# Another order for the opening of a LayerNorm, 2D-FFT filter and gated MLP kernel, with a later chunk's statistics put ahead of a transform

## The chip, the cores and the metric

The kernel runs on one core of one Trainium2 chip. The metric is device time in microseconds (us), the median over runs of the same program; lower is better. The engines are named as in the profile: PE (TensorE, matrix products), PEld (its weight loads), DVE (VectorE), ACT (ScalarE), POOL (GpSimd) and SP (SyncE, whose queue issues the DMA loads, stores and transposes). Each engine works through its own list in order; a step that needs another engine's result waits for a semaphore, and so does everything listed behind it on that engine.

## The reference

The input x has 2048 rows and 448 columns, the inner width is 1792, and everything is in float32:

```python
xn = (x - mean(x)) / sqrt(var(x) + 1e-5)                 # per row
X = rfft2(xn, axes=(-2, -1)) * (w_r + 1j * w_i)
spectral = irfft2(X, s=(2048, 448), axes=(-2, -1))
gate = xn @ W_gate                                       # 448 x 1792
gate = gate * (gate > 0)
mlp = (gate * (xn @ W_up)) @ W_down                      # 1792 x 448
return x + spectral + mlp
```

## The kernel before

**Precision.** All large products run on PE in float16. Each operand is split into a hi part (rounded to float16) and a lo part (what the rounding left), and a product is three passes, hi·hi, lo·hi and hi·lo, added up in PSUM. So for each operand some engine makes hi, and then DVE makes lo by a subtraction that reads hi.

**Tiling.** The 2048 rows are 16 tiles of 128, numbered 0 to 15. Four tiles with the same remainder modulo 4 make a chunk of 512 rows; the chunks are used in the order 0, 2, 1, 3 (`CHUNKS`), so chunk 1 is the third. T0, T2, T1 and T3 are their normalized and transposed forms, what PE streams in the MLP. The gate and up weights come in 14 slabs of 128 inner columns, each as a gate half (g0) and an up half (g1): W0g0, W0g1, W1g0 and so on.

**Steps for one row tile n.** `lx` loads it (SP, `load_xr`). `st` is `ln_stats`: `bn_stats` and `bn_aggr` on DVE, lines 255 and 258 (the profile calls the tile `y`, or `g` for tile 4, which travels in another buffer). `sq` and `rs` are `ln_sd` (one small operation on ACT, line 266) and `ln_rstd` (a chain of four small ones on DVE, 271 to 275). `xn` normalizes on DVE (297), `ax` does the same on ACT (295). `hi` makes the hi part on ACT from the normalized tile (306), or fused with the normalization (`hx` and `hi` stand for the two forms, 304 and 306; for tiles 0, 4, 8 and 12 `hi` is the fused one). `cp` copies two pieces on POOL (310, 311). `lo` is two subtractions on DVE (321 for 384 columns, 322 for 64). The tile then goes to T in one of two ways. For the first chunk PE transposes it: `tpA` the three hi blocks, `tpB` the five other blocks, lo ones among them, all eight into one PSUM tile, and `vevA`/`vevB` or `aevA`/`aevB` bring three and five blocks to SBUF, by DVE or by ACT (345). For the other chunks a DMA transposes it (`dm`, `ln_dma`, line 330 on SP).

**Steps for one weight half.** `lw` loads the next one (SP, line 231, into one of eight `wst` buffers). `wsq` squares it on ACT and sums along the row (185, output `junk`), `parW` sums over the partitions on POOL (188), `wscW` derives a power-of-two scale (two small DVE operations, 191 and 195), `whi` makes hi on ACT (699), `wlo` makes lo on DVE (703) and lets the `wst` buffer go.

**Products.** PSUM has three pairs of banks for the MLP. The products of slab 0 and slab 1 with T0 are cut into small pieces, since neither T0 nor the weights are complete: `hh`, `lh`, `hl` for slab 0 and `ah`, `bh`, `ch` for slab 1, 256 columns at a time (757, 128x256). `gu2g0`, `gu2g1` and on are whole halves of 512 columns. Slab 2 takes the bank pair of slab 0 again: gate after `re0` (ReLU on ACT, 799) has read it, up after `tm0` (the product with up on DVE, 803). `gh` and `gl` split the result again (807, 811), and line 834 is the product with the down weights. `warm` and `kw` are products of a constant (line 1094) whose result nobody reads.

**What sets the order.** The opening, up to about 40 us, is a string of 238 names, `OPENING`. Its steps are issued word by word in a scope where no scheduler moves them, so the string gives each engine's list. What follows is placed by a planner: MLP units in a fixed order, and between them background steps from a list `bg` that is filled in lines 909 to 960: loads of the third chunk's rows, the forward transform of chunk 0 (`fft_chunk`, `f_dft` and on; on DVE lines 385 to 455), its rows, `ln_chunk(1)` (statistics, reciprocal deviation, normalization, lo and transposes of the third chunk), and so on. Each entry has a DVE cost, and the planner spreads the list over the units by those costs. `t_ninth` and `n0` copy what sticks out of T's blocks into a further tile Tl by four small DMAs (351, 352).

Of the kernel before, what the change touches and what calls it, by code (L numbers as in the profile page):

```python
# [33 lines left out]
tpB12 wsqW3g0 vevB8 wloW1g0 ah10 wsqW3g1 vevB12 ah01 parW2 ah11 lwd2 wloW1g1 wscW2 bh00 hl11 hl01 lx14 whiW2g0
bh01 hp0 ch10 whiW2g1 lw st2 bh11 st6 re0 wloW2g0 bh10 wsqW4g1 ch00 ch11 tm0 gu2g0 parW3 wscW3 st14 wsqW4g0
whiW3g0 wloW2g1 ch01 ly0 parW4 wscW4 whiW3g1 wloW3g1 lw wsqW5g1 lx10 whiW4g0 wloW3g0 gh0 re1 st10 gu2g1 tm1 hp2
sqC rsC wsqW5g0 xn6 gu3g0 re2 parW5 wscW5 whiW5g0 tm2 wloW4g0 xn10 xn14 hx14 lwd4 hx6 lo6 hi10 whiW5g1 lo10
gu4g0 hx2 wloW5g0 whiW4g1 cp14 xn2 wdq0 gl0 cp10 gu3g1 wloW4g1 lo14 lwd3 wdq4 wdq2 cp2 re3 tm3 cp6 wloW5g1 gh1
gu4g1 gh2 wdq3 ly12 lo2 hp4 wdq1 wdp wdsc wdh4 dm10 gl1 re4 ly8 wdh3 gl2 gu5g1 tm4 gh4 dm14 gl4 dm6 gu5g0 dm2
re5 lfd gz0g0 wdl3 gz0g1 tm5 hp6 gh3 gl3 rz0 gh5 wdl4 gl5 wdh1 wdl1 wdh2 wdl2 n0 wdh0 wdl0 gz1g0 tz0 gz1g1 rz1  # L40
hz0 tz1 hz1 lz0 lz1
# [103 lines left out]
def tile_gfnet_reglu(ctx: ExitStack, tc: tile.TileContext, x, xr, xi, wgu, wd, wf, c_fd, c_fm, c_im, c_row, c_id,  # L145
# [106 lines left out]
    def ln_stats(q, j):  # L252
        n2 = q + 4 * j
        st = ft([128, 6], F32, "bst", 2)
        V.bn_stats(st, xr_t[n2])  # L255
# [12 lines left out]
    def ln_rstd(q, js=(0, 1, 2, 3), bias=False):
        w, m = rst[q, js[0]]
        r0, t, r, nm = (w[:, i] for i in range(4))  # L270
        V.scalar_tensor_tensor(t, m[:, :, 1], 1e-5, r0, op0=OP.add, op1=OP.mult)
        V.scalar_tensor_tensor(t, t, -0.5 * 2048, r0, op0=OP.mult, op1=OP.mult)
        V.scalar_tensor_tensor(r, t, 1.5 * 2048, r0, op0=OP.add, op1=OP.mult)
        if bias:
            V.scalar_tensor_tensor(nm, m[:, :, 0], -1.0, r, op0=OP.mult, op1=OP.mult)
# [4 lines left out]
    tts = [ft([128, 8, 128], F16, f"tt{i}") for i in range(4)]  # L280
# [15 lines left out]
        else:  # L296
            V.tensor_scalar(xn[n2], xr_t[n2], mean, r, op0=OP.subtract, op1=OP.mult)

    def ln_hi(n2, fused=False):
        new_tt(n2)  # L300
        o = tt[n2].rearrange("p a b -> p (a b)")[:, 0:D]
        r, nm, _ = rst[n2 % 4, n2 // 4]
        if fused:
            A.activation(o, xr_t[n2], AF.Identity, scale=r, bias=nm)  # L304
        else:
            A.activation(o, xn[n2], AF.Copy)
# [387 lines left out]
        for i, k in enumerate(gs):  # L694
            wsc[f, k] = sc[:, i:i + 1]

    def w_hi(f, g):
# [1 line left out]
        A.activation(w[:, 0:4, :], wst[f, g], AF.Copy, scale=wsc[f, g])  # L699
# [392 lines left out]
    def keep_warm(n):  # L1092
        for _ in range(n):
            P.matmul(wps, warm[:, 0:128], warm, start=True, stop=True)
# [192 lines left out]
```

## Time and profile before

| | us |
|---|---|
| median of 3 runs | 442.78 |
| lowest to highest | 442.63 to 443.31 |
| span of the profiled execution | 440.9 |
| busy in it: PE | 435.7 |
| DVE | 382.3 |
| ACT | 184.5 |
| POOL | 29.4 |

The profile is one execution. Its span, 440.9 us, is counted from its first instruction to its last, and what the device needs around it is not part of it, so it stands 1.9 us under the median. Starts in the rows are us from the span's start; a row gives start, duration, engine, line, operation, output <- input, shape, how many were merged into it, and in brackets how long the engine sat idle and who released it. The duration of one instruction overlaps the next one's start on the same engine, so the distance between starts is the cost when they stand back to back. Semaphore events of the trace give the landing of each piece of a load, which the views print only indirectly.

### The profile page before, as it was taken

The page shows a single profiled execution, that of the slowest core. Times are in us where ns is not written, and L with a number is a line of the kernel's source. Part 1 is how long each engine was busy: PE and PEld are TensorE (multiplying, and loading weights), DVE is VectorE, ACT ScalarE, POOL GpSimd, SP SyncE. Part 2 cuts the span into 40 slices and gives each one's busy share as a digit, 9 for nine tenths or more (in the row PEclk, how much of TensorE's full clock was granted, in tenths as well). Part 3 has the DMA queues.
Part 4 walks back from the last instruction along what each step waited for, and adds up shares of the span by engine and source line. Part 5 has one row for each costly group of instructions (what it writes and reads, how often), then busy time and mean ns, then how long its engine had stood idle before and what let it go on. Part 6 is the DMA issues. An engine that isn't in the chain of part 4 may idle for free.

```text
span 440.9 us, 7429 instructions
## 1 busy us (share of the span) xinstructions
PE 435.7 (99%) x2641; PEld 221.9 (50%) x2641; DVE 382.3 (87%) x957; ACT 184.5 (42%) x396; POOL 29.4 (7%) x75
## 2 busy tenths in 40 slices
PE   8999999999999999999999999999999999999996
PEld 3744464554445545444545444444545555555664
DVE  6998496989887879999999999988997989798644
ACT  6995427392457236144023467233113332243220
POOL 3230002011100040000000020000000000000000
PEclk9999999999999999999999999999999999999999
DMA  7929895304111123332220210001111121210212
GB/s 256 301 91 198 269 364 172 70 2 107 59 49 50 47 76 119 94 118 84 86 84 1 84 43 1 0 1 42 44 43 49 54 91 34 72 55 33 89 51 104
DMA packets 37613, 39.55 MB, mean 90 GB/s; under 512 B 16535, under 2 KB 33353, under 8 KB 37577
## 3 DMA queue, kind: packets, MB, share of 16 engines
q1 hardware_dynamic: 37576, 39.09, 29.1%
q8 instruction: 20, 0.33, 0.3%
q14 instruction: 17, 0.13, 0.1%
HBM read 24.38 MB, written 3.67 MB: 64 GB/s over the span
## 4 chain that ended last, share of the span: by engine, by line
PE 90%; DVE 4%; ACT 3%; DMA 1%; issue 1%; SPq 0%; POOL 0%; ACTq 0%
PE bank L757 49%; PE bank L834 27%; PE bank L764 3%; PE fx L648 2%; PE fx L369 2%; PE fx L667 2%; PE fx L406 2%; PE bank L853 2%; ACT wt L699 1%; DMA T<-tt 1%; ACT junk L185 1%; DVE bst L255 1%; DVE wt L703 1%; DMA y<-in_xr 1%; ACT tt L304 1%
## 5 line engine op out<-in xcount | busy, mean ns | idle before, releaser
L757 PE MATMUL bank<-T,wt 128*128 128x512 f16 (+1 forms) x1160 | 252.7, 372 | 0.6 <-DVE T L345 0.5
L757 PEld LDWEIGHTS <-wt 128*128 128x128 f16 x1160 | 110.9, 98 | 127.6 <-issue 7.2
L834 PE MATMUL bank<-wdt,h 128*128 128x448 f16 x624 | 122.4, 352 | 0.0
L834 PEld LDWEIGHTS <-h 128*128 128x128 f16 x624 | 60.5, 98 | 55.1
L799 ACT ACTIVATE g<-bank 128x512 f32<-128x512 f32 x56 | 33.0, 591 | 80.4 <-PE bank L757 45.2
L807 ACT ACTIVATE h<-g 128x512 f16<-128x512 f32 x56 | 35.0, 627 | 70.1 <-DVE g L803 70.0
L803 DVE SCALAR_TENSOR_TENSOR g<-bank,g 128x512 f32<-128x512 f32 x56 | 38.2, 683 | 11.9 <-PE bank L757 6.8
L811 DVE TENSOR_TENSOR h<-g,h 128x512 f16<-128x512 f32 x56 | 38.1, 684 | 6.7 <-ACT h L807 6.4
L840 DVE SCALAR_TENSOR_TENSOR xy<-bank,dsc,xy 128x448 f32<-128x448 f32 x44 | 29.8, 676 | 5.5 <-PE bank L834 5.2
L632 ACT ACTIVATE vt<-y,fsc 128x456 f16<-128x456 f32 x15 | 10.1, 674 | 34.5 <-issue 14.0
L699 ACT ACTIVATE wt<-wst,wsc 128x512 f16<-128x512 f32 x28 | 19.3, 713 | 11.1 <-DVE wsc L195 10.3
L703 DVE SCALAR_TENSOR_TENSOR wt<-wst,wsc,wt 128x512 f16<-128x512 f32 x28 | 20.4, 742 | 0.5 <-ACT wt L699 0.3
L672 DVE SCALAR_TENSOR_TENSOR xy<-fx,fsc,xy 128x448 f32<-128x448 f32 x16 | 10.8, 680 | 10.9 <-PE fx L667 10.9
L188 POOL PARTITION_ALL_REDUCE wm<-wm x15 | 10.5, 697 | 139.9 <-ACT junk L185 136.4
L185 ACT ACTIVATE junk<-wst 128x512 bf16<-128x512 f32 x28 | 17.2, 616 | 0.0
L397 ACT ACTIVATE Xh<-X 128x456 f16<-128x456 f32 x16 | 9.3, 579 | 16.4 <-DVE X L395 9.3
L764 PE MATMUL bank<-T,wt 64*128 64x512 f16 x112 | 15.6, 380 | 0.0
L400 DVE TENSOR_TENSOR Xh<-X,Xh 128x456 f16<-128x456 f32 x16 | 9.8, 624 | 4.9 <-ACT Xh L397 4.9
L648 PE MATMUL fx<-im,vt 128*128 128x128 f16 x192 | 13.3, 219 | 0.0
L667 PEld LDWEIGHTS <-pgh 114*128 114x128 f16 x192 | 10.9, 98 | 3.8 <-issue 0.8
L648 PEld LDWEIGHTS <-vt 128*128 128x128 f16 x192 | 11.6, 98 | 1.3
L406 PE MATMUL fx<-Xh,fm 128*128 128x456 f16 x48 | 12.2, 356 | 0.0
(168 smaller groups left out, 480.1 us busy)
## 6 DMA issues: line engine op xcount, KB each, us to landing
wst<-in_wgu SPq DMA_DIRECT2D x28, 256.0 KB
sw<-y SPq DMA_DIRECT2D x56, 112.2 KB
wf<-in_wf SPq DMA_DIRECT2D x16, 228.0 KB
xy<-in_x SPq DMA_DIRECT2D x16, 224.0 KB
y<-in_xr SPq DMA_DIRECT2D x15, 224.0 KB
out<-xy SPq DMA_DIRECT2D x15, 224.0 KB
wdst<-in_wd SPq DMA_DIRECT2D x14, 224.0 KB
fm<-in_c_fm SPq DMA_DIRECT2D x4, 256.0 KB
```

What stands on the lines that cost most here:

```text
L185: A.activation(mt([128, 512], BF16, "junk", 2)[:, 0:src.shape[-1]], src, AF.Square, scale=SQ, accum_out=acc)
L648: P.matmul(o, v[:, h, w], m[:, c, :], start=(i == 0), stop=(i == 2), skip_group_check=True)
L699: A.activation(w[:, 0:4, :], wst[f, g], AF.Copy, scale=wsc[f, g])
L703: V.scalar_tensor_tensor(w[:, 4:8, :], st, sc, w[:, 0:4, :], op0=OP.mult, op1=OP.subtract)
L757: last["P"] = P.matmul(hps[f, q][g][:, cs], wt[f, g][:, a, :], Tq[q][:, b, cs], start=(start and i == 0), stop=(stop and i == len(seq) - 1 ...
L764: m = P.matmul(hps[f, q][g][:, 0:512], wt[f, g][rows, 7, :], Tq[q][rows, b, :], start=start, stop=stop).ins
L799: last["A"] = A.activation(g1s[f, q], hps[f, q][0], AF.Relu, scale=2.0 ** -22).ins
L803: last["V"] = V.scalar_tensor_tensor(g1, hps[f, q][1], 2.0 ** -22, g1, op0=OP.mult, op1=OP.mult).ins
L807: A.activation(ht[f, q][:, 0, :], g1s[f, q], AF.Copy)
L811: V.tensor_tensor(h[:, 1, :], g1s.pop((f, q)), h[:, 0, :], op=OP.subtract)
L834: last["P"] = P.matmul(ps[:, 0:D], ht[f, q][:, a, js], wdt[f][:, b, :], start=(i == 0), stop=(i == n - 1)).ins
L840: last["V"] = V.scalar_tensor_tensor(xy[:, n2, :], dps[n2][:, 0:D], dsc[:, g:g + 1], xy[:, n2, :], op0=OP.mult, op1=OP.add).ins
```

## The change

All 238 steps of the opening stay, some in another form, and the loads stay in the order they had on SP up to the last few; the order of the steps on the engines is a new one. The first words, before and after, show the kind of edit:

```diff
-OPENING = """lx0 st0 lx4 st4 sqA rsA ax4 hi0 lx8 st8 lx12 xn0 lw cp0 lw lw lw hx4 warm tpA4 st12 tpA0 lo0 lx6 sqB rsB cp4 lo4
-wsqW0g0 tpB0 kw4 tpB4 wsqW0g1 lx2 hi8 parW0g0 wscW0g0 lwd1 whiW0g0 vevA0 parW0g1 wscW0g1 vevA4 hh00 tpA8 whiW0g1
+OPENING = """lx0 lx4 st0 st4 warm18 lx8 lx12 sqA rsA lw vh4 cp4 lw ax0 wsqW0g0 xn4 st12 tpA4 lo4 hx0 parW0g0 tpA0 lw cp0 tpB4 lo0
+tpB0 lw wscW0g0 lx6 wsqW0g1 vevA0 aevA4 parW0g1 wsqW1g0 warm4 lx2 wsqW1g1 aevB4 vevB0 lwd1 wscW0g1 vwW0g0 whiW0g1
...
-    rst = {}
+    rst, rsb = {}, {}
...
-        w = ft([128, 4, 4], F32, "rs", 3)
+        w = ft([128, 4, 4], F32, "rs", 4)
...
-    def ln_hi(n2, fused=False):
+    def ln_hi(n2, fused=False, eng=None):
...
-        if fused:
+        if eng is not None:
+            eng.tensor_scalar(o, xr_t[n2], mean, r, op0=OP.subtract, op1=OP.mult)
+        elif fused:
...
-    def w_hi(f, g):
+    def w_hi(f, g, eng=None):
...
-        A.activation(w[:, 0:4, :], wst[f, g], AF.Copy, scale=wsc[f, g])
+        if eng is None:
+            A.activation(w[:, 0:4, :], wst[f, g], AF.Copy, scale=wsc[f, g])
+        else:
+            eng.tensor_scalar(w[:, 0:4, :], wst[f, g], wsc[f, g], None, op0=OP.mult)
...
-    def ln_chunk(q):
+    def ln_head(q):
         for j in range(4):
             add(0.73, ln_stats, q, j)
         add(0.0, ln_sd, q)
         add(0.75, ln_rstd, q, (0, 1, 2, 3), True)
+
+    def ln_rows(q):
...
     add(0.0, t_ninth, 2)
+    ln_head(1)
     fft_chunk(0)
     fft_rows(0)
-    ln_chunk(1)
+    ln_rows(1)
...
-    ln_chunk(3)
+    ln_head(3)
+    ln_rows(3)
```

Three kinds of step change engine or form. `vh4`, `vh8` and `vh10` make a row tile's hi part on DVE. `vwW0g0`, `vwW2g1` and `vwW4g0` make a weight half's hi part on DVE. `aevA4`, `aevB4`, `aevA8` and `aevB8` evict transposes on ACT instead of DVE, and several normalizations (`xn`) become ACT's (`ax`), while tile 4's becomes DVE's. The constant products are 18 and 4 where they were 21 and 4. `n0`, the four small DMAs for T0, comes earlier. The rest of the diff gives names to further forms of these steps that the string does not use. Outside the opening, `ln_head(1)`, the third chunk's statistics and reciprocal deviation, is taken out of `ln_chunk(1)` and put ahead of the first transform.

ACT's list from the first normalization on, before (`tt_100` is row tile 0's hi and lo, `tt_101` row tile 4's; `junk,wm<-wst` is the square of a weight half):

```order
L295 ACTIVATE y_67<-g_127,rs 128x448
L304 ACTIVATE tt_100<-y_66,rs 128x448
L306 ACTIVATE tt_101<-y_67 128x448
L266 ACTIVATE rs<-mv,eps 128x2
L185 ACTIVATE junk,wm<-wst 128x512 x2
L304 ACTIVATE tt_102<-y_68,rs 128x448
L699 ACTIVATE wt<-wst,wsc 128x512 x2
```

And now (`tt_101` is row tile 0's here, and the L347 row the eviction of transposes of tile 4):

```order
L297 ACTIVATE y_69<-y_66,rs 128x448
L183 ACTIVATE junk,wm<-wst 128x512
L310 ACTIVATE tt_101<-y_69 128x448
L183 ACTIVATE junk,wm<-wst 128x512
L347 ACTIVATE T_62<-fx 128x3x128
L183 ACTIVATE junk,wm<-wst 128x512 x2
L347 ACTIVATE T_62<-fx 128x5x128
L704 ACTIVATE wt<-wst,wsc 128x512
```

The first square of a weight half now stands ahead of row tile 0's hi part, and row tile 4's hi part has left ACT.

DVE's list up to the operands of the first product, before (from the first lo pair's successor on):

```order
L321 TENSOR_TENSOR tt_101<-y_67,tt_101 128x384
L322 TENSOR_TENSOR tt_101<-y_67,tt_101 128x64
L191 TENSOR_SCALAR eg<-wm 128x1
L195 TENSOR_SCALAR wsc<-eg 128x1
L345 COPY T_62<-fx 128x3x128
```

And now (L706 is `vwW0g0`, the first weight half's hi part):

```order
L325 TENSOR_TENSOR tt_101<-y_69,tt_101 128x384
L326 TENSOR_TENSOR tt_101<-y_69,tt_101 128x64
L189 TENSOR_SCALAR eg<-wm 128x1
L193 TENSOR_SCALAR wsc<-eg 128x1
L349 COPY T_62<-fx 128x3x128
L349 COPY T_62<-fx 128x5x128
L189 TENSOR_SCALAR eg<-wm 128x1
L193 TENSOR_SCALAR wsc<-eg 128x1
L706 TENSOR_SCALAR wt<-wst,wsc 128x512
L253 BN_STATS bst<-y_67 128x6
```

Row tile 0's five-block eviction and the second half's scale now stand ahead of the first weight hi part, which was ACT's.

DVE's list around `tm0` (the row with the bank pair's second bank, `bank_112`), before:

```order
L258 BN_AGGR mv<-bst 128x2
L703 SCALAR_TENSOR_TENSOR wt<-wst,wsc,wt 128x512
L803 SCALAR_TENSOR_TENSOR g_404<-bank_112,g_404 128x512
L191 TENSOR_SCALAR eg<-wm 128x2
L195 TENSOR_SCALAR wsc<-eg 128x2
L255 BN_STATS bst<-y_75 128x6
```

And now (`y_75` is row tile 14 and `y_76` row tile 10, so its row is `st10`):

```order
L710 SCALAR_TENSOR_TENSOR wt<-wst,wsc,wt 128x512
L253 BN_STATS bst<-y_75 128x6
L256 BN_AGGR mv<-bst 128x2
L710 SCALAR_TENSOR_TENSOR wt<-wst,wsc,wt 128x512
L253 BN_STATS bst<-y_76 128x6
L256 BN_AGGR mv<-bst 128x2
L810 SCALAR_TENSOR_TENSOR g_428<-bank_112,g_428 128x512
```

The statistics of row tiles 14 and 10 have moved from behind `tm0` to ahead of it.

More of the change, by code (lines that the diff above doesn't have):

```diff
@@ L34 @@
[L34 to L38, printed above, removed]
@@ L39 @@
[L39 to L41 removed]
+OPENING = """lx0 lx4 st0 st4 warm18 lx8 lx12 sqA rsA lw vh4 cp4 lw ax0 wsqW0g0 xn4 st12 tpA4 lo4 hx0 parW0g0 tpA0 lw cp0 tpB4 lo0
+tpB0 lw wscW0g0 lx6 wsqW0g1 vevA0 aevA4 parW0g1 wsqW1g0 warm4 lx2 wsqW1g1 aevB4 vevB0 lwd1 wscW0g1 vwW0g0 whiW0g1
+parW1 st8 sqB wscW1 hh00 wloW0g0 whiW1g1 hl00 ly4 lw rsB vh8 hh10 hl10 lw whiW1g0 lh00 lw ah10 cp8 ch10 ah00 tpA8 hi12
@@ new lines @@
+wloW1g1 tpA12 wloW0g1 bh10 ax12 ch00 aevA8 lw vevA12 wloW1g0 lw lh10 bh11 lw cp12 hh11 wsqW2g1 lo12 bh00 ax8 wsqW2g0
+lo8 tpB12 lwd0 parW2 wsqW3g1 bh01 lwd2 hh01 lx14 vevB12 tpB8 wsqW3g0 wscW2 st6 ah11 parW3 ah01 st2 aevB8 lw whiW2g0
+vwW2g1 lh11 lh01 wsqW4g1 hl11 wsqW4g0 wscW3 hl01 wloW2g0 st14 ly0 hp0 ch01 lw re0 wloW2g1 parW4 lx10 st10 ch11 wsqW5g0
+lwd4 wdq0 tm0 gu2g0 re1 whiW3g1 sqC tm1 wscW4 whiW3g0 gh0 wloW3g1 wloW3g0 lwd3 gu2g1 gl0 wsqW5g1 parW5 n0 ly12 whiW4g1
+hp2 gh1 rsC vwW4g0 re2 ax6 ax10 gu3g1 tm2 wscW5 gu3g0 hi6 gh2 whiW5g1 wloW4g0 lo6 vh10 wloW4g1 ax2 wloW5g1 cp6 hi2
@@ L42 @@
+whiW5g0 cp2 gu4g0 re3 wdq3 hx14 cp10 lo10 gl1 ly8 ax14 lo2 wloW5g0 dm6 gu4g1 cp14 dm10 tm3 hp4 wdq1 wdq2 gu5g1 lo14
+wdq4 wdp gl2 dm2 re4 gu5g0 tm4 gh4 dm14 gh3 wdsc wdh3 wdh0 gl4 re5 tm5 wdh1 wdh2 gz0g0 gz0g1 wdl1 hp6 wdh4 wdl2 gz1g0
+gl3 wdl4 rz0 gh5 gz1g1 rz1 tz0 gl5 wdl3 wdl0 tz1 lfd hz0 hz1 lz0 lz1
 """
@@ L255, in ln_stats @@
         V.bn_stats(st, xr_t[n2])
-        if j == 0:
+        if q not in mv:
             mv[q] = ft([128, 4, 2], F32, "mv", 2)
         V.bn_aggr(mv[q][:, j, :], st)
-    rst = {}
+    rst, rsb = {}, {}
     def ln_sd(q, js=(0, 1, 2, 3)):
-        w = ft([128, 4, 4], F32, "rs", 3)
+        w = ft([128, 4, 4], F32, "rs", 4)
         n = len(js)
-        rst[q, js[0]] = w[:, :, 0:n], mv[q][:, js[0]:js[-1] + 1, :]
-        A.activation(w[:, 0, 0:n], rst[q, js[0]][1][:, :, 1], AF.Abs_reciprocal_sqrt, bias=eps)
+        rsb[q, js[0]] = w[:, :, 0:n], mv[q][:, js[0]:js[-1] + 1, :]
+        A.activation(w[:, 0, 0:n], rsb[q, js[0]][1][:, :, 1], AF.Abs_reciprocal_sqrt, bias=eps)
     def ln_rstd(q, js=(0, 1, 2, 3), bias=False):
-        w, m = rst[q, js[0]]
+        w, m = rsb[q, js[0]]
         r0, t, r, nm = (w[:, i] for i in range(4))
@@ L274, in ln_rstd, with ln_bias @@
         if bias:
-            V.scalar_tensor_tensor(nm, m[:, :, 0], -1.0, r, op0=OP.mult, op1=OP.mult)
+            ln_bias(q, js)
         for i, j in enumerate(js):
             rst[q, j] = r[:, i:i + 1], nm[:, i:i + 1], m[:, i, 0:1]
+    def ln_bias(q, js):
+        w, m = rsb[q, js[0]]
+        V.scalar_tensor_tensor(w[:, 3], m[:, :, 0], -1.0, w[:, 2], op0=OP.mult, op1=OP.mult)
     xn, tt, xn_b = {}, {}, {}
@@ L1096, in tile_gfnet_reglu @@
     pieces = {"lfd": lambda: nc.sync.dma_start(fd_t, c_fd),
-              "lw": load_wn, "warm": lambda: keep_warm(NWARM),
-              **{f"kw{n}": (lambda n=n: keep_warm(n)) for n in (1, 3, 4)},
+              "lw": load_wn, **{f"warm{n}": (lambda n=n: keep_warm(n)) for n in range(1, 25)},
               "wdp": lambda: wd_sum(len(groups[0])),
@@ L1110, in tile_gfnet_reglu @@
             n2 = q + 4 * j
+            piece(f"sq{n2}", ln_sd, q, (j,))
+            piece(f"rs{n2}", ln_rstd, q, (j,))
+            piece(f"nm{n2}", ln_bias, q, (j,))
             for tag, fn, *a in (("lx", load_xr), ("ly", load_x), ("st", ln_stats, j), ("xn", ln_xn),
-                                ("hi", ln_hi, c == 0), ("hx", ln_hi, c == 1), ("ax", ln_xn, True), ("cp", ln_copy), ("lo", ln_lo), ("dm", ln_dma),
+                                ("hi", ln_hi, c == 0), ("hx", ln_hi, c == 1), ("ax", ln_xn, True), ("cp", ln_copy), ("lo", ln_lo),
+                                ("vh", ln_hi, False, V), ("dm", ln_dma),
                                 ("tpA", ln_tp, (0, 1, 2)), ("tpB", ln_tp, (4, 5, 6, 3, 7))):
@@ L1151, in tile_gfnet_reglu @@
             piece(f"whiW{f}g{g}", w_hi, f, g)
+            piece(f"vwW{f}g{g}", w_hi, f, g, V)
             piece(f"wloW{f}g{g}", w_lo, f, g)
@@ L1154, in tile_gfnet_reglu @@
             if f == 0:
+                for j in range(2):
+                    for tag, sq in (("hq", seq1[0:3]), ("lq", seq1[3:6]), ("kq", seq2)):
+                        piece(f"{tag}{g}{j}", gu_full, f, q, (g,), slice(128 * j, 128 * j + 128), tag == "hq" and j == 0,
+                              False, sq)
                 piece(f"parW{f}g{g}", w_sum, f, (g,))
```

5 lines of the change are left out of this document (1 added, 4 removed).

## The prediction

> **What bounds the kernel now.** I read the page's busy shares and chain first, then the windows, then each engine's timeline over the opening.
>
> ```profile
> PE 435.7 (99%) x2641; PEld 221.9 (50%) x2641; DVE 382.3 (87%) x957; ACT 184.5 (42%) x396; POOL 29.4 (7%) x75
> PE 90%; DVE 4%; ACT 3%; DMA 1%; issue 1%; SPq 0%; POOL 0%; ACTq 0%
> ```
>
> TensorE (PE) is busy 435.7 of 440.9 us. The windows (length, then busy time of PE, PEld, DVE, ACT, POOL) say where the rest lies:
>
> ```profile
> 0.00:10.00 10.00, 8.78 (x37) 3.78 (x38) 6.28 (x25) 5.74 (x12) 3.76 (x17) 1.00 0.77 241
> 10.00:20.00 10.00, 9.51 (x93) 7.55 (x92) 9.44 (x29) 9.22 (x22) 2.50 (x7) 1.00 0.97 330
> 20.00:30.00 10.00, 10.00 (x56) 4.94 (x55) 9.72 (x28) 9.37 (x21) 1.81 (x5) 1.00 0.34 118
> ...
> 40.00:50.00 10.00, 9.89 (x49) 4.16 (x48) 6.51 (x12) 5.29 (x11) 0.00 (x0) 1.00 0.95 305
> ...
> 80.00:90.00 10.00, 10.00 (x81) 5.32 (x79) 10.00 (x34) 4.55 (x11) 0.00 (x0) 1.00 0.09 24
> ```
>
> From 20 us PE is full, so the main phase can give back almost nothing. The start decides; PE's timeline there:
>
> ```profile
> 1.22 7.46 PE L1094 MATMUL bank<-row_t 128*128 128x512 f16 x21 [1.22 <-DVE row_t L1166]
> 8.52 0.78 PE L337 MATMUL fx<-g,tt 128*128 128x128 f16 x11
> 9.13 1.03 PE L1094 MATMUL bank<-row_t 128*128 128x512 f16 x4
> 9.99 0.44 PE L337 MATMUL fx<-g,tt 128*128 128x128 f16 x5
> 10.93 0.49 PE L757 MATMUL bank<-T,wt 128*128 128x256 f16 x3 [0.49 <-DVE T L345]
> ```
>
> L1094 is warming on constants, L337 the first transposes, L757 the first product: useful work starts at 10.93. After it PE runs nearly without a break, so every microsecond by which the first product moves goes straight into the end, unless a later stall swallows it.
>
> **First product: +0.9.** What comes before it on ScalarE (ACT), SyncE's DMA queue and VectorE (DVE):
>
> ```profile
> 6.02 0.76 ACT L295 ACTIVATE y<-g,rs 128x448 f32<-128x448 f32 x1 [0.81 <-DVE rs L275]
> 6.69 0.75 ACT L304 ACTIVATE tt<-y,rs 128x448 f16<-128x448 f32 x1
> 7.34 0.56 ACT L306 ACTIVATE tt<-y 128x448 f16<-128x448 f32 x1
> ...
> 8.13 0.61 ACT L185 ACTIVATE junk<-wst 128x512 bf16<-128x512 f32 x1
> 8.74 0.61 ACT L185 ACTIVATE junk<-wst 128x512 bf16<-128x512 f32 x1
> ...
> 10.13 1.33 ACT L699 ACTIVATE wt<-wst,wsc 128x512 f16<-128x512 f32 x2
> ```
>
> ```profile
> 2.60 1.85 SPq L231 DMA_DIRECT2D wst<-in_wgu  x4
> ...
> 6.29 0.61 SPq L214 DMA_DIRECT2D xy<-in_x  x1
> 8.01 5.33 SPq L231 DMA_DIRECT2D wst<-in_wgu  x6
> ```
>
> ```profile
> 5.90 0.62 DVE L255 BATCH_NORM_STATS2 bst<-y 128x6 f32<-128x448 f32 x1
> ...
> 6.66 0.48 DVE L297 TENSOR_SCALAR y<-y,mv,rs 128x448 f32<-128x448 f32 x1
> ...
> 7.81 0.58 DVE L321 TENSOR_TENSOR tt<-y,tt 128x384 f16<-128x384 f32 x1
> ...
> 8.47 0.19 DVE L271 SCALAR_TENSOR_TENSOR rs<-mv,rs 128x2 f32<-128x2 f32 x1
> ...
> 9.16 0.55 DVE L321 TENSOR_TENSOR tt<-y,tt 128x384 f16<-128x384 f32 x1
> ...
> 9.76 0.15 DVE L191 TENSOR_SCALAR eg<-wm 128x1 uint32<-128x1 uint32 x1
> ...
> 10.01 0.35 DVE L345 COPY T<-fx 128x384 f16<-128x384 f16 x1
> 10.28 0.14 DVE L191 TENSOR_SCALAR eg<-wm 128x1 uint32<-128x1 uint32 x1
> ```
>
> Before, ACT finishes both rows' hi parts (L304, L306) by 7.90 and only then squares the first weight slab (L185 at 8.13). The change puts that square between row 0's normalization and row 0's hi part, on an engine that works in order. So the row waits for the weights. When do they land? SyncE's next weight load, queued behind the last x load (6.90), starts only at 8.01: its queue slot is that of the first slab, whose last piece the trace's semaphore events put at 7.99. The load's place in the queue is unchanged, so I take 8.0 again.
>
> The walk, by start-to-start distances of the same rows: normalization at 6.02 as before; square 8.02; hi 0.61 later (8.74−8.13), 8.63; its end 9.19 (0.56). The lo pair on DVE follows at 9.22; its first part (0.55) releases the first of the five transposes that need lo, near 9.84, and the five take 0.44 (PE's row at 9.99): 10.28. The first eviction of that row, three blocks of hi, shares its PSUM tile with those five, and in the new program it waits for the tile's last transpose: 10.32 (before, a three-block eviction ran at 10.01). Behind it on DVE, in order: the five-block eviction +0.27 (10.28−10.01) at 10.59; that one takes 0.40 to the next start (0.27 for three blocks, and two more of 128 at a column a nanosecond or less, half of it hidden: an estimate), so the second slab's scale stands at 10.99 and, being two small operations of 0.25 together (10.01−9.76), ends the wait at 11.24; then the first slab's hi part, which now is DVE's. That operation is not in the trace; beside the L297 row above stands:
>
> ```profile
> 11.59 1.40 DVE L703 SCALAR_TENSOR_TENSOR wt<-wst,wsc,wt 128x512 f16<-128x512 f32 x2
> ```
>
> L297, the same operation on 448 elements, took 0.48; two-source ones on 512 took 1.40 a pair, some 0.74 each. I take 0.55 (0.48 scaled by 512/448), bounds 0.48 and 0.74. It ends 11.79; semaphore to PE 0.04: **first product 11.83 against 10.93, +0.90** (+0.83 to +1.09 by the bounds). PE waits through this, so the three dropped warm matmuls (0.22 each) gain nothing.
>
> Whether ACT's new evictions of the other row's tiles matter: an ACT read of PSUM of 512 took 0.58 (quoted below), so 384 and 640 lie near 0.49 and 0.70; they end at 10.3 and 12.2, the second within 0.1 of its first reader. Before, PE lost some 0.1 each at 11.36 and 14.77; I count the small stalls 11 to 15 equal. The Trainium skill ("ScalarE: Activation LUTs", on the cost of an ACTIVATE) gives 186 ns and 0.833 ns an element, so 0.51 and 0.72 here; the trace's 0.58 for 512 lies just under its 0.61. By it nothing in the sum moves.
>
> **The first reuse of a bank: +0.4.** PE, then the load that st10 reads, then DVE, then ACT:
>
> ```profile
> 19.04 6.89 PE L757 MATMUL bank<-T,wt 128*128 128x256 f16 x42
> ```
>
> ```profile
> 18.65 0.43 SPq L225 DMA_DIRECT2D y<-in_xr  x1
> ```
>
> ```profile
> 20.52 0.68 DVE L803 SCALAR_TENSOR_TENSOR g<-bank,g 128x512 f32<-128x512 f32 x1
> ...
> 24.39 0.62 DVE L255 BATCH_NORM_STATS2 bst<-y 128x6 f32<-128x448 f32 x1
> ```
>
> ```profile
> 19.76 0.58 ACT L799 ACTIVATE g<-bank 128x512 f32<-128x512 f32 x1
> ```
>
> L803 (tm0) frees the up bank; gu2g1 writes it next. Of the 42 products from 19.04, eighteen of 256 columns (0.110 apart) come before gu2g0 at 21.02. In the new order a further four (ch01) come first, 0.44: 21.46, and 22.36 with the +0.90. gu2g0's ten of 512 columns (0.216) end at 24.52, when gu2g1 wants the bank. DVE reaches tm0 later than before: twenty steps stand between the hi part at 11.24 and tm0. By distances from start to start: five statistics of 0.76 (6.66−5.90) are 3.80, six weight lo parts of 0.66 (1.40−0.74) 3.96, a chain of four small ones 0.69 (9.16−8.47), two hi parts 0.39 (0.48 less the 0.09 by which neighbours overlap) and 0.50, evictions 0.27 and 0.40, two lo pairs 0.66 (8.47−7.81) 1.32, three scale pairs of two slabs some 0.3 each 0.9: 12.2. From 11.74, when the hi part lets the next start, tm0 starts at 23.9 if DVE never waits, ends 24.6, and PE loses 0.1. But st10 now stands ahead of tm0, and it waits for the load at 18.65, which before was read only at 24.39 (semaphore events: landed 23.16). It is issued at about the same time, with other loads shifted some 2 us around it; I put its landing between 22 and 24, thus the loss between 0 and 1.2. I take 0.4.
>
> **T2's and T1's transposes: −0.28 and −0.13.** The chain and PE's weight loads:
>
> ```profile
> 36.42 3.87 DMA T<-tt
> ...
> 40.33 4.49 PE bank L757 x20
> ```
>
> ```profile
> 80.02 0.10 PEld L369 LDWEIGHTS <-Tl 128*128 128x128 f16 x1
> 80.22 0.56 PEld L757 LDWEIGHTS <-wt 128*128 128x128 f16 x4
> ```
>
> PE stood 0.28 (starts 0.49 apart instead of 0.216) for the last transpose of T2, landed 40.29. The new order issues it near 36.5, so it lands at about the same time, but PE comes 1.3 later: gone. At 80 a load follows its forerunner by 0.20 where 0.05 would do; PE's matmul starts 0.13 late, for T1, whose transposes are the last to land ahead of it. With the third chunk's statistics ahead of the transform, and no row DMAs ahead of them on SyncE, they can start some 10 us sooner: gone. What hides the moved statistics (four of 0.76 on DVE and a chain of four small ones): they begin near 40, where DVE is busy 6.5 of 10 (window row) and nothing behind them is due at once. Without that cover each would hold up what frees a bank by its 0.76. From there to the end PE's order is the same, and the tail with it.
>
> Sum: +0.90 +0.4 −0.28 −0.13 = **+0.89**. Span 440.9 → 441.8. The median 442.78 lies 1.88 above the profiled span; the same distance gives **443.7**. A measurement of this kernel can tell about 0.2% (0.9 us) from no change.
>
> **Rivals.**
>
> *A: the weights land earlier.* Only three of the 16 pieces came after 6.81. If all come by 6.78, the square follows the normalization directly, hi ends 7.95, and the lo pair waits for DVE (about 8.2). The same chain then gives a first product at 10.8 (8.2 in place of 9.22 for the pair), 10.4 if the pair needn't wait: −0.5 to −0.1. It decides from a landing at 7.1 down. With both transposes' gain: about −0.6, so 442.2, between −0.9 and 0; not slower. Against it: the queue and what is on it have not changed, and SyncE's stop until 8.01 is in this profile. 25%.
>
> *B: a queue behind a wait.* Both ACT and DVE are over 90% full from 10 to 30 (window rows); st10's load lands late, or another in-order wait is added to it, and gu2g1 and the product after each lose 0.5 to 1. +1.6 to +2.5: 445.0. 16%.
>
> *C: PE slows down.* PE idles 1.2 us before row 0's transposes (7.87+0.17 to 9.24), and once more before the first product. If that drops the clock to the start's pace, the 21 warm matmuls' row prices it: 7.46 us where 21×0.217 is 4.6, so up to 2.9 more. For it: the start. Against it: 0.49 of idle at 10.93 was followed by full pace. +2.9 and the sum: 446. 4%. The Trainium skill ("TensorE: Matmul & The Clock Gate", Part 1: The HAM clock gate) lets the clock fall only after an idle window of some 3.4 us; by it C is out. No run here shows a gap that long, and the slow start here (about 5.5 us) is longer than its one window.
>
> **Numbers.** Forecast 55%: +0.2 to +1.6, half of it over +0.9. Slower by over 0.2%: 0.27+0.16+0.04 = 0.47. Same: 0.28 of the forecast and 0.14 of A: 0.42. Faster: A's far end, 0.11. Range 442.0 to 445.1: it leaves out A's end, B's upper half and C.
>
> **What would show it.** Right: the square (ACT, `junk`) starts near 8.0 with idle time ahead of it, hi after it, the first L757-kind product near 11.8; a PE wait on `g` from DVE near 24.5; no transpose wait at 40 and 80. Wrong: hi done before 8.4, or the first product under 11.2 (A); any later PE stall over 0.5 (B); products 0.22 apart for 256 columns (C).

## The result, and the profile after

The changed kernel takes 449.19 us (448.44 to 451.03, 5 runs) where the kernel before takes 443.31 (442.63 to 443.85, 5 runs, same chip): ratio 1.0139, interval 1.0123 to 1.0154, so 5.9 us slower. The forecast was 443.7 with a range to 445.1. The sign that had the largest chance came out; the size is outside the range.

The profiled execution spans 447.2 us, 6.3 more than before. Busy shares and chain from the page after:

```profile
PE 437.3 (98%) x2638; PEld 222.2 (50%) x2638; DVE 381.0 (85%) x954; ACT 186.1 (42%) x399; POOL 34.9 (8%) x75
PE 81%; DVE 10%; DMA 5%; issue 1%; ACT 1%; SPq 1%; DVEq 0%; ACTq 0%
```

PE's share of the chain fell from 90% to 81%. DVE and DMA now have 10% and 5% of it, so somewhere PE waits for them. POOL is busy 5.5 us longer with the same 75 instructions. PE's waits in sum, with count and longest:

```profile
PE bank L771 <- DVE g L810: 2.5, 2, 2.2
PE fx L341 <- ACT tt L310: 1.3, 1, 1.3
PE bank L764 <- ACT g L806: 0.8, 1, 0.8
PE bank L764 <- DVE wt L706: 0.6, 1, 0.6
PE fx L341 <- POOL tt L315: 0.3, 1, 0.3
```

The largest one is on a line that did not wait at all before (L764 there, L771 here: the products with Tl). Where they lie, in PE's timeline of the opening:

```profile
1.22 6.72 PE L1105 MATMUL bank<-row_t 128*128 128x512 f16 x18 [1.22 <-DVE row_t L1185]
7.79 0.33 PE L341 MATMUL fx<-g,tt 128*128 128x128 f16 x3
9.42 1.08 PE L341 MATMUL fx<-g,tt 128*128 128x128 f16 x13 [1.31 <-ACT tt L310]
10.34 1.03 PE L1105 MATMUL bank<-row_t 128*128 128x512 f16 x4
11.99 1.04 PE L764 MATMUL bank<-T,wt 128*128 128x256 f16 x7 [0.63 <-DVE wt L706]
```

The first product comes at 11.99 (10.93 before). Later in PE's timeline:

```profile
37.69 4.26 PE L764 MATMUL bank<-T,wt 128*128 128x512 f16 x19
42.71 3.61 PE L764 MATMUL bank<-T,wt 128*128 128x512 f16 x16 [0.76 <-ACT g L806]
...
204.00 0.82 PE L771 MATMUL bank<-T,wt 64*128 64x512 f16 x6 [0.35 <-DVE g L810]
...
231.60 1.18 PE L771 MATMUL bank<-T,wt 64*128 64x512 f16 x6 [2.18 <-DVE g L810]
232.72 6.20 PE L764 MATMUL bank<-T,wt 128*128 128x512 f16 x22
```

and the same place before:

```profile
226.71 0.82 PE L764 MATMUL bank<-T,wt 64*128 64x512 f16 x6
227.46 4.92 PE L757 MATMUL bank<-T,wt 128*128 128x512 f16 x22
```

Two things are new there. PE stands 2.18 us. Then the same 28 products take 1.18 + 6.20 where they took 0.82 + 4.92: 1.64 us for a slower pace, start to start up to 427 ns for 512 columns instead of 216. Windows of the changed kernel show the clock that PE was granted (the first number behind the five busy times, as a share of full speed):

```profile
228.53:231.94 3.41, 1.23 (x9) 0.51 (x8) 3.41 (x8) 0.36 (x1) 0.00 (x0) 1.00 0.46 147
231.94:235.35 3.41, 3.41 (x13) 0.97 (x8) 3.41 (x8) 0.87 (x2) 0.00 (x0) 0.50 0.24 77
```

Half the clock was granted for 3.41 us, right behind 3.41 us in which PE was busy for only 1.23.

The difference between the two traces, by distances from start to start on PE:

| place | us |
|---|---|
| first product, 10.93 to 11.99 | +1.06 |
| small stalls at 12 to 13 | +0.06 |
| 17.9: last transpose of the first chunk, waits for POOL's copy | +0.41 |
| 24.9: `gu2g1` behind `tm0` | +0.25 |
| 41.6: 0.92 of standing, 0.28 before | +0.64 |
| 80: T1's transposes | −0.13 |
| 204: waits for L810 | +0.35 |
| 229 to 239: 2.18 idle, 1.64 slow pace | +3.82 |
| rest | −0.2 |
| span | +6.3 |

The opening and T2 cost 2.3; more than half of the loss comes at 200 to 239, far from anything that the new string holds.

### The profile page after: what moved, and what is told of

Read it like the earlier page. It is cut to its first block, busy times and chain, and to the rows that moved or that the text cites. A ratio compares the mean times of both kernels' runs of the same rounds, so it can differ in the third digit from the quotient of the medians.

```text
span 447.2 us, 7419 instructions
## 1 busy us (share of the span) xinstructions
PE 437.3 (98%) x2638; PEld 222.2 (50%) x2638; DVE 381.0 (85%) x954; ACT 186.1 (42%) x399; POOL 34.9 (8%) x75
## 4 chain that ended last, share of the span: by engine, by line
PE 81%; DVE 10%; DMA 5%; issue 1%; ACT 1%; SPq 1%; DVEq 0%; ACTq 0%
PE bank L764 45%; PE bank L841 23%; PE bank L771 3%; PE fx L652 2%; PE fx L373 2%; PE fx L671 2%; PE fx L410 2%; PE bank L860 2%; DMA wf<-in_wf 2%; DMA wst<-in_wgu 1%; DMA y<-in_xr 1%; DVE y L524 1%; DVE g L810 1%; DVE xy L847 1%; DMA sw<-yx 1%
## 5 line engine op out<-in xcount | busy, mean ns | idle before, releaser
L764 PE MATMUL bank<-T,wt 128*128 128x512 f16 (+1 forms) x1160 | 254.0, 373 | 1.5 <-ACT g L806 0.8
L764 PEld LDWEIGHTS <-wt 128*128 128x128 f16 x1160 | 111.5, 98 | 130.3 <-issue 10.0
L814 ACT ACTIVATE h<-g 128x512 f16<-128x512 f32 x56 | 35.0, 626 | 73.1 <-DVE g L810 73.0
L810 DVE SCALAR_TENSOR_TENSOR g<-bank,g 128x512 f32<-128x512 f32 x56 | 38.3, 686 | 17.6 <-ACT g L806 8.9
L818 DVE TENSOR_TENSOR h<-g,h 128x512 f16<-128x512 f32 x56 | 38.4, 686 | 8.3 <-ACT h L814 8.2
L704 ACT ACTIVATE wt<-wst,wsc 128x512 f16<-128x512 f32 x25 | 17.4, 712 | 13.2 <-DVE wsc L193 9.9
L186 POOL PARTITION_ALL_REDUCE wm<-wm x15 | 11.4, 768 | 138.3 <-ACT junk L183 138.3
L676 DVE SCALAR_TENSOR_TENSOR xy<-fx,fsc,xy 128x448 f32<-128x448 f32 x16 | 10.8, 681 | 10.9 <-PE fx L671 10.9
L771 PE MATMUL bank<-T,wt 64*128 64x512 f16 x112 | 15.9, 386 | 2.5 <-DVE g L810 2.5
L297 ACT ACTIVATE y<-y,rs 128x448 f32<-128x448 f32 x15 | 10.7, 752 | 3.4 <-DVE rs L279 2.1
```

The source lines that it names most:

```text
L764: last["P"] = P.matmul(hps[f, q][g][:, cs], wt[f, g][:, a, :], Tq[q][:, b, cs], start=(start and i == 0), stop=(stop and i == len(seq) - 1 ...
L771: m = P.matmul(hps[f, q][g][:, 0:512], wt[f, g][rows, 7, :], Tq[q][rows, b, :], start=start, stop=stop).ins
L810: last["V"] = V.scalar_tensor_tensor(g1, hps[f, q][1], 2.0 ** -22, g1, op0=OP.mult, op1=OP.mult).ins
L814: A.activation(ht[f, q][:, 0, :], g1s[f, q], AF.Copy)
L818: V.tensor_tensor(h[:, 1, :], g1s.pop((f, q)), h[:, 0, :], op=OP.subtract)
```

## The experiments

Three theories had to be told apart. **The opening theory**: the first product's delay is the price, as the forecast had it. **The late theory (L)**: the planner put the spectral work of the main phase in other places, and that loses time at 200 to 239. **The T2 theory (T)**: what ends the opening is T2's last transpose, held up by POOL. The expectations also name further rivals, each explained where it stands. All times are medians; each ratio is against the kernel before on the same chip, and kernels measured on different chips (the last three on another) are compared by these ratios.

### The third chunk's statistics alone

The old opening in the changed kernel (with `warm21` and `warm4` for the old `warm` and `kw4`):

```diff
-OPENING = """lx0 lx4 st0 st4 warm18 lx8 lx12 sqA rsA lw vh4 cp4 lw ax0 wsqW0g0 ...
+OPENING = """lx0 st0 lx4 st4 sqA rsA ax4 hi0 lx8 st8 lx12 xn0 lw cp0 lw lw lw hx4 warm21 tpA4 ...
```

> The opening of before, with the third chunk's statistics ahead of the first transform as after. After's trace loses 2.4 us up to 60 us (first product +1.06, a POOL copy at 18 +0.41, the up bank at 25 +0.25, a gate bank at 42 +0.92, T2's wait gone -0.28) and about 4 us more between 200 and 236 (DVE idle on late loads, the product of the up half waiting for DVE, and eight products at half pace behind it). Theory S: the statistics ahead of the transform push the whole spectral chain back by their 3.7 us of DVE, and that is what comes due at 200 to 236; then this kernel is some 4 us slower than before (447.0 to 447.6), the first product stays at 10.9, and PE waits near 229. Rival O: the late stall is the opening's doing, by what it leaves to the scheduler; then this kernel is within 0.5 us of before (T1's 0.13 gone).

Measured: 442.61 (441.98 to 443.39, 10 runs), ratio 0.9993 (0.998 to 1.0005). Its waits on PE:

```profile
PE bank L765 <- DVE T L350: 0.7, 1, 0.7
PE bank L772 <- DVE g L811: 0.2, 1, 0.2
```

No wait on T2 or T1 and none of 2 us: the statistics ahead of the transform cost nothing by themselves, and with the old opening the main phase is sound. So the new string, or what it does together with the planner, makes the loss.

### The new opening alone

```diff
-    ln_head(1)
     fft_chunk(0)
     fft_rows(0)
+    ln_head(1)
```

> The new opening, with the third chunk's statistics back behind the first transform. Theory S: the 2.4 us up to 60 us stay, the 4 us at 200 to 236 go: 445.5 to 446.0. Rival O: 449, as after. Should the two halves not add up (with the old opening and the statistics ahead), each needs the other.

Measured: 445.26 (444.37 to 446.39, 5 runs), ratio 1.0054 (1.0036 to 1.0073). The late loss is gone. In the profiled execution the first weight half had landed at 6.98, the case of rival A, and the first product came at 10.81, ahead of before's 10.93. Still:

```profile
38.65 2.54 PE L764 MATMUL bank<-T,wt 128*128 128x512 f16 x11
42.56 2.75 PE L764 MATMUL bank<-T,wt 128*128 128x512 f16 x12 [1.37 <-DMA T<-tt]
```

PE gets to T2 early and stands 1.37 for its transposes, which land at 42.42 (semaphore events). An early first product is given back at T2. Since moving the entry in the list also changes the order of the main phase, this run alone doesn't say what removed the late loss.

### The row's hi part ahead of the first square

```diff
-... lw ax0 wsqW0g0 xn4 st12 tpA4 lo4 hx0 parW0g0 ...
+... lw ax0 hx0 wsqW0g0 xn4 st12 tpA4 lo4 parW0g0 ...
```

> After, with row tile 0's hi part on ACT ahead of the first square of a weight half, which waited for its load until 8.15. The step as predicted (a hi part stuck behind a late load): first product from 11.99 to about 10.9, and as PE is full behind it about 1 us less: 448.1 or so. Rival: the chain through the evictions and the second half's scale on DVE is as late by itself, since the second square now comes later: first product stays over 11.6 and the time within 0.4 of after.

Measured: 449.2 (448.82 to 449.3, 4 runs), ratio 1.014 (1.0125 to 1.0155): as the changed kernel, though its first product is 0.89 earlier in the profile. Most of that is the weights, which landed at 7.44 in this execution (8.16 in the changed kernel's). PE:

```profile
11.10 2.16 PE L764 MATMUL bank<-T,wt 128*128 128x256 f16 x17 [0.63 <-ACT T L347]
...
43.04 2.32 PE L764 MATMUL bank<-T,wt 128*128 128x512 f16 x10 [1.21 <-ACT wdt L738]
```

In all seven profiles of the new opening with the hi part behind the square the first product comes 3.83 or 3.84 after the weights have landed, and in the four with the hi part ahead of it (this one and three below) 3.56 to 3.66. So the edit itself is worth some 0.2, and the rival was near the truth: with the weights at 8.16 the first product would, by that, still come at about 11.8. The row keeps waiting for the weights on POOL, where its two copies (8.86 and 9.01 here) stand behind `parW0g0`, which needs the square.

The opening theory fails as the price of the whole: the wait behind `tm0` at 24 grows from 0.25 to 1.02, the one at 41 from 0.92 to 1.38, and together they eat the earlier start, wherever it came from. The late loss stays (2.04 of idle at 229.7, then the slow pace).

### The last ReLU ahead of the down weights

At 41.6 the named releaser is ACT's `re5`, which stands behind two hi parts of the down weights; the first of these waits for DVE's scale.

```diff
-... gh3 wdsc wdh3 wdh0 gl4 re5 tm5 ...
+... gh3 re5 wdsc wdh3 wdh0 gl4 tm5 ...
```

> After, with the ReLU re5 put ahead of the down weights' scale and their first two hi parts on ACT. In after PE stands 0.92 at 42 until re5 has read the bank. If re5 alone holds it, 0.8 to 0.9 go (448.3). But T2's last transpose was issued at 39.8 and its first piece landed at 42.4, so the rival is that T2 takes over: only 0.2 go, and PE then waits for a DMA.

Measured: 445.24 (444.51 to 445.43, 4 runs), ratio 1.0054 (1.0036 to 1.0071), 4 us under the changed kernel where under 1 us was expected. A miss, and its cause is in the written order: this edit too changes the planner's placing of the main phase, and the late loss is gone. At 41 PE now waits 1.34 for T2 itself, landing at 42.19: the ReLU and T2 had ended within 0.02 of each other, and without one the other decides.

### Only the planner's cost

The opening's string stays word for word; one cost of the background list changes, and with it only the order of the main phase.

```diff
-            add(0.73, ln_stats, q, j)
+            add(0.86, ln_stats, q, j)
```

> After with one number of the planner changed: it books a row tile's statistics at 0.86 us instead of 0.73. No instruction and nothing of the opening changes; only the order of the main phase does. In the written DVE order the third chunk's first spectral sum stands behind 19 MLP units instead of after's 20 and the first filter products behind 26 instead of 28, as they do in the kernels that lost nothing late. Theory L (after's late loss lies in this order, not in the opening nor in the statistics as such): no PE wait near 204 and 229, no half pace behind it, some 4 us less: 444.9 to 446. Rival: the late loss comes from how late the opening ends or from the statistics' 3.7 us: 449, as after.

Measured: 445.77 (445.08 to 445.99, 4 runs), ratio 1.0062 (1.0043 to 1.0081). PE where it stood 2.18:

```profile
229.56 0.82 PE L771 MATMUL bank<-T,wt 64*128 64x512 f16 x6
230.31 4.92 PE L764 MATMUL bank<-T,wt 128*128 128x512 f16 x22
```

No wait, full pace, and 3.4 us less than the changed kernel with the same opening and the same instructions: the late loss lies in the order of the main phase, and L is shown. The other direction, 0.60:

> The same number at 0.60. The written order keeps the spectral chain where after has it (20 units, 28). Theory L: the late loss stays, 448.5 to 449.7. Rival (any nudge to the planner frees it): about 445.

Measured: 448.9 (448.65 to 449.1, 4 runs), ratio 1.0134 (1.0119 to 1.0149). L810 is waited for four times, 3.4 us in sum. PE at the same place:

```profile
231.78 0.82 PE L771 MATMUL bank<-T,wt 64*128 64x512 f16 x6 [1.64 <-DVE g L810]
232.53 4.92 PE L764 MATMUL bank<-T,wt 128*128 128x512 f16 x22
```

Here full pace follows after 1.64 of idle.

What the two orders differ in: in DVE's list the third chunk's first sum of the transform (the fifth of eight such sums in all) stands behind 18 products with up (`tm`, L810) in the changed kernel, in the one with the row's hi part first and in the 0.60 one, and behind 17 before and in every other kernel of this case (the expectations count units of the program, 20 and 19). Those three kernels have the late loss, and no other has it. On the chip the sum starts at 137.6 in the changed kernel, 131.9 before, 130.6 in the kernel with the old opening, and 132.9 with cost 0.86. From there the spectral chain runs some 5 to 7 us behind that of the 0.86 kernel. How it reaches PE, back from the stall: DVE, ACT and SP of the changed kernel:

```profile
217.55 0.69 DVE L818 TENSOR_TENSOR h<-g,h 128x512 f16<-128x512 f32 x1 [2.17 <-ACT h L814]
```

```profile
215.81 0.30 ACT L517 ACTIVATE wf<-wf 128x114 f32<-128x114 f32 x1 [4.96 <-DMA wf<-in_wf]
...
216.91 0.61 ACT L814 ACTIVATE h<-g 128x512 f16<-128x512 f32 x1
```

```profile
211.75 0.90 SPq L513 DMA_DIRECT2D wf<-in_wf  x2
```

The filter load `wf` stands on SP behind the spectral rows' transfers, is issued at 211.75 (202.27 with cost 0.86, 201.64 before) and lands at 215.8. ACT works in order: the sign flip L517 waits for it, the gate's hi part L814 stands behind L517, and DVE's L818 behind L814 stands 2.17. DVE then works without a break until L810 at 230.86, which PE has waited for since 229.4: 2.17 lost on DVE, 2.18 on PE. In the other two kernels with this loss the same two waits are 2.03 and 2.04 (row's hi part first) and 1.64 and 1.64 (0.60). This path is read from the traces; no run moved that one load alone. Before, the same flip on ACT waited for nothing:

```profile
207.72 0.47 ACT L513 ACTIVATE wf<-wf 128x114 f32<-128x114 f32 x2
```

### The opening without the late loss

With cost 0.86, the row's hi part first again:

```diff
-            add(0.73, ln_stats, q, j)
+            add(0.86, ln_stats, q, j)
...
-... lw ax0 wsqW0g0 xn4 st12 tpA4 lo4 hx0 parW0g0 ...
+... lw ax0 hx0 wsqW0g0 xn4 st12 tpA4 lo4 parW0g0 ...
```

> The planner's number at 0.86, and row tile 0's hi part ahead of the first weight square on ACT. If the first product is on the path, as the prediction had it, the time falls by what the first product gains against the kernel with the number alone, 0.1 to 1.0 by when the weights land. Theory T: T2's transposes and the ReLU re5 hold PE at 41 to 42.5 whatever comes before, since other engines set their time, so the first product is worth nothing: within 0.3 of the kernel with the number alone, and the PE wait near 41 longer by what the start gained.

Measured: 445.13 (444.9 to 446.62, 4 runs), ratio 1.0057 (1.0035 to 1.0078). Inconclusive: 0.6 under the kernel with 0.86 alone, and the intervals overlap. Its profile is of the slowest of the runs, with the weights at 8.03 and the first product at 11.68 (7.90 and 11.73 with 0.86 alone), and PE waits 1.3 behind `tm0` and 0.8 for T2.

### T2 and POOL

Why is T2 late? POOL's copies in the changed kernel, each of 48 or 64 columns:

```profile
16.04 0.22 POOL L314 COPY tt<-tt 128x48 f16<-128x48 f16 x1
16.20 2.03 POOL L315 COPY tt<-tt 128x64 f16<-128x64 f16 x1
...
33.25 1.88 POOL L314 COPY tt<-tt 128x48 f16<-128x48 f16 x1 [1.67 <-ACT tt L310]
35.07 0.73 POOL L315 COPY tt<-tt 128x64 f16<-128x64 f16 x1
...
35.91 0.23 POOL L315 COPY tt<-tt 128x64 f16<-128x64 f16 x1
36.09 0.22 POOL L314 COPY tt<-tt 128x48 f16<-128x48 f16 x1
36.25 1.35 POOL L315 COPY tt<-tt 128x64 f16<-128x64 f16 x1
```

and DVE beside the last three:

```profile
35.63 0.68 DVE L810 SCALAR_TENSOR_TENSOR g<-bank,g 128x512 f32<-128x512 f32 x1
36.23 0.54 DVE L325 TENSOR_TENSOR tt<-y,tt 128x384 f16<-128x384 f32 x1
36.69 0.22 DVE L326 TENSOR_TENSOR tt<-y,tt 128x64 f16<-128x64 f32 x1
36.83 0.68 DVE L818 TENSOR_TENSOR h<-g,h 128x512 f16<-128x512 f32 x1
```

A copy takes 0.22 or 0.23 beside L810, whose one source is a PSUM bank, and 1.35 beside L325, L326 and L818, whose two sources are both in SBUF and which follow one another without a gap. In the two traces every copy that took over 0.4 ran beside such an operation. The Trainium skill ("SBUF — State Buffer", SBUF: two separate sides) says that VectorE and GpSimd share a pair of ports under an exclusive lock, which the operation that starts first holds to its end, a VectorE one with two SBUF inputs among them. The trace agrees, and adds that POOL didn't get in between operations that stood back to back: the copy at 16.20 outlasted five of them. The copies at 33.25 and 35.07 are row tile 2's; row tile 10's stand behind them, and SP, whose next transpose is row tile 10's, waits for those:

```profile
SPq L334 <- POOL tt L314: 2.4, 1, 2.4
```

The SP queue is in order, so the four transposes of T2 are issued at 31.64, 36.17, 37.51 and 39.76 (30.80, 33.71, 35.06 and 36.42 before), and the last lands at 42.57 (40.29). Of the 3.3 us by which the last is issued later, 2.5 were there at the second; the rest is the issue of the third, which took 2.09 (1.25 before). Experiment: row tile 10's copies ahead of tile 2's, out of the longest runs of such operations; `re5` early as well; cost 0.86.

```diff
-... wloW5g1 cp6 hi2 whiW5g0 cp2 gu4g0 re3 wdq3 hx14 cp10 lo10 ...
+... wloW5g1 cp6 cp10 hi2 whiW5g0 cp2 gu4g0 re3 wdq3 hx14 lo10 ...
...
-... gh3 wdsc wdh3 wdh0 gl4 re5 tm5 ...
+... gh3 re5 wdsc wdh3 wdh0 gl4 tm5 ...
```

> The planner's number at 0.86, re5 ahead of the down weights' hi parts, and on POOL tile 10's copies ahead of tile 2's, which in after took 1.9 and 0.7 instead of 0.2 each and held tile 10's transpose. Theory T: T2's transposes are issued in a queue that waits for POOL, so their last landing comes 1 to 2 us sooner than 42.4, PE's wait near 41 shrinks from 1.5 to about 0.3, and the time is 443.9 to 444.8. Rival: POOL's copies are held up by DVE wherever they stand; nothing gained, 445.2 to 445.9.

Measured: 444.29 (443.1 to 445.35, 5 runs), ratio 1.0032 (1.0012 to 1.0052). T2's last transpose is issued at 37.19 and lands at 41.10; PE doesn't wait for it. The swap of the copies without the ReLU's:

> The kernel of e5 (planner cost 0.86, 445.77) with row tile 10's two POOL copies ahead of tile 2's, and re5 left behind the down weights. If the POOL copies alone hold T2's last transpose: it is issued near 37 to 38 and lands by 41.5, PE waits near 41 for the ReLU re5 on ACT instead, 0.3 to 0.9, and the time is 445.0, between e5 and e8 (444.3). If the ReLU's place is what e8 gained by: as e5, 445.8.

Measured: 443.98 (443.57 to 445.51, 12 runs), ratio 1.0027 (1.0016 to 1.0038). POOL in this kernel:

```profile
32.95 0.55 POOL L314 COPY tt<-tt 128x48 f16<-128x48 f16 x1
33.45 0.23 POOL L315 COPY tt<-tt 128x64 f16<-128x64 f16 x1
35.23 0.34 POOL L314 COPY tt<-tt 128x48 f16<-128x48 f16 x1 [1.55 <-ACT tt L308]
35.52 0.23 POOL L315 COPY tt<-tt 128x64 f16<-128x64 f16 x1
```

By the ratios the swap alone brings some 1.5 us against the kernel with 0.86 alone (1.0062), give or take 1.0, and no less than the two edits together. That the copies held T2 back is shown: PE doesn't stand at 41 at all. How much it is worth is not shown so finely. The two profiles are 1.8 apart (spans 443.7 and 441.9); 0.8 of that is the wait for T2, and 1.0 is a shorter wait behind `tm0` near 25, ahead of anything that the swap touches. The expected wait for the ReLU did not come. All four kernels with 0.86 and the swap have the same order in the main phase as the one with 0.86 alone.

### What is left in the opening

The kernel with both edits, and the row's hi part first; then also `st10` back behind `tm0` and `tm1`:

```diff
-... ax0 wsqW0g0 xn4 st12 tpA4 lo4 hx0 parW0g0 ...
+... ax0 hx0 wsqW0g0 xn4 st12 tpA4 lo4 parW0g0 ...
...
-... parW4 lx10 st10 ch11 wsqW5g0 lwd4 wdq0 tm0 gu2g0 re1 whiW3g1 sqC tm1 ...
+... parW4 lx10 ch11 wsqW5g0 lwd4 wdq0 tm0 gu2g0 re1 whiW3g1 tm1 st10 sqC ...
```

> The kernel of e8 with row tile 0's hi part (hx0) put ahead of the first weight square; the main phase's order is that of e5 and e8. Theory S (the opening's end is set by whichever of first product, st10's load and T2 comes last; in e8 T2 is no longer late): the first product comes 0.6 to 0.9 earlier than in e8's 11.75, and since tm0 still stands behind st10, whose load lands at 23 to 24.8, some of it is lost there; 443.7, span about 442.0, with a tm0 wait of 0.6 to 1.0 near 24. Theory F (the first product's delay was the opening's price, as the prediction had it): all of it counts, 443.4 or under, no larger wait at 24. If the row's hi part gains nothing at all, 444.3.

> The kernel of e9 with the statistics of row tile 10 (st10) put back behind tm0 and tm1. Theory S: the last of the three waits goes, tm0 starts without waiting for a load: 0.6 to 1.0 under e9, 442.9, level with the kernel before or just under it; PE's waits between 20 and 30 under 0.3 in sum. Theory F: nothing waits there to begin with, same as e9.

Measured: 444.1 (443.71 to 444.56, 11 runs), ratio 1.0022 (1.0013 to 1.0031), and 443.98 (443.36 to 444.57, 11 runs), ratio 1.0019 (1.001 to 1.0028). In the profiles the steps do what they should: first product at 10.98 and 0.98 lost behind `tm0`; then nothing lost behind `tm0`, spans 442.6, 442.2, 441.5. In the medians the last four kernels lie within 0.3 us, which these runs can't tell apart, and both expected sizes (443.7 or less, 442.9) were missed. None of them beats the kernel before; the new opening stays about 0.8 to 1.4 us behind. The three spans are those of single executions, the last of them the shortest of its 11. The spans of all runs have medians of 442.4, 442.2 and 442.1 (442.1 with the swap alone, about 441.0 before), which go with the median times. So most of the gain that the profiles suggest isn't there. Executions differ by themselves: the first weight half landed between 6.98 and 8.16 in the profiled ones, whatever the kernel.

## Why the prediction was wrong, point by point

**First product: right in size and in the chain, too simple in the cause.** ACT and DVE of the changed kernel:

```profile
6.41 0.76 ACT L297 ACTIVATE y<-y,rs 128x448 f32<-128x448 f32 x1 [0.82 <-DVE rs L279]
8.18 0.63 ACT L183 ACTIVATE junk<-wst 128x512 bf16<-128x512 f32 x1 [1.01 <-DMA wst<-in_wgu]
...
8.81 0.56 ACT L310 ACTIVATE tt<-y 128x448 f16<-128x448 f32 x1
```

```profile
9.40 0.56 DVE L325 TENSOR_TENSOR tt<-y,tt 128x384 f16<-128x384 f32 x1 [0.85 <-ACT tt L310]
...
11.46 0.48 DVE L706 TENSOR_SCALAR wt<-wst,wsc 128x512 f16<-128x512 f32 x1
```

The square waits 1.01 for the weights and starts at 8.18 (8.02 forecast), hi follows at 8.81 (8.63), the lo pair at 9.40 (9.22). The new form of the weight's hi part takes 0.48, the lower bound. Product at 11.99 against 11.83: +1.06 for +0.90, the difference being the weights' landing (8.16 for 7.99). But the square ahead of the hi part is only some 0.2 of it, as the kernels with the hi part first show (3.6 from the landing to the first product in place of 3.83; before, 2.94): the row also waits for the weights through POOL, which the walk left out. And the argument lacked that this delay buys time for what follows: at 24 and at 41 the next operands were late anyway, so an execution with a first product 0.89 earlier gained nothing.

**First reuse of a bank: right.** 0.25 for 0.4; the load of `st10` landed at 23.9, inside the 22 to 24, and DVE stood 0.42 for it. (The working's twenty steps ahead of `tm0` are 21 by its own terms; their sum holds.)

**T2: wrong.** "The new order issues it near 36.5" is a step read from places in a list. It was issued at 39.76: the two copies ahead of row tile 10's took 1.88 and 0.73 where before those of T2 took 0.28 to 0.73, and SP stood 2.4 for POOL. "Gone" became 0.64 worse. POOL was in no term of the sum, and the same effect at 16.20 cost the 0.41 at 17.9. T1's −0.13 came as forecast.

**"From there to the end PE's order is the same, and the tail with it": wrong, and the costliest step.** PE's order behind the opening is not the same: of the 628 transform products in its list after 45 us, over 200 stand between other MLP products than before. That alone costs nothing, since it holds for the old opening with the statistics ahead too. But DVE's, ACT's and SP's lists moved with it, one product with up more comes ahead of the third chunk's first sum, and behind that the filter load comes too late. Why the placing of the background work depends on the opening was not followed up, but little is enough: moving the one word `re5` changed it as well. About 4 us of the 6.3 lie here, 3.4 by the kernel that changes only the cost, in a term that the sum put at nothing.

**The rivals.** A's case came in single executions: with the weights at 6.98 the first product stood at 10.81, where A had worked out 10.8, but the time did not follow: that execution took 444.86. B's kind of wait came, an in-order queue behind a late operand, at 41 and 215; where B put it the changed kernel lost only 0.25, but the kernels with cost 0.86 lost up to 1.44 there, behind `tm0`. C's mechanism came too: 1.64 us of slow pace behind an idle stretch, at 231, not in the opening. By the Trainium skill ("TensorE: Matmul & The Clock Gate", Part 1: The HAM clock gate) C was set aside, since the clock should fall only after an idle window of some 3.4 us. Here it fell to 0.50 after 2.18 of idle, and in the run with the row's hi part first after 2.04; the measurement decides.

The kernel with the new opening, the main phase's good order and the copies out of the way (443.98) is 0.96 above before in the medians, close to the +0.89. That is in part luck: this kernel has another order on POOL than the one that was forecast, and it still loses the 0.41 near 17.9, which is in none of the sum's terms.

## What to carry to other kernels

Where a planner places what follows an edit, compare the lists of every engine to the end of the program, and don't take it that only the edited stretch has moved: 4 us lay some 190 us behind the new opening, where a filter load that was issued some 10 us later held up ACT, DVE and then PE. A delay at the start is a price only if no later operand is late as well, so ask of each later wait when its own operand would be there. And a small copy on POOL is not cheap where DVE runs operations with two SBUF sources back to back.
